# A cached-attention decode kernel: the last weight rows on eight DMA engines by the GpSimd queue, and values that trail keys by three groups

## The chip, the cores and the metric

One core of one Trainium2 chip runs the whole kernel. The metric is the device time of one execution in microseconds (us). The runs of the kernel before agree within 0.3%, so differences of a few tenths of a per cent need several rounds. The kernel before takes 195.49 us (median; 195.32 to 195.64).

Some words are used throughout. PE is the engine for matrix products (PEld in a profile is its loading of weights), DVE and ACT work on elements, GpSimd (POOL) is a fourth engine, and sync (SP) here only issues loads and stores. A *queue* is what an engine issues loads on (sync, activation, GpSimd). A *DMA engine* is one of the sixteen units that by the page move the bytes (in the kernel before a fetch puts one engine about 1.6 us behind).

## The reference, cut to what matters

```
B, D = 8, 448          # eight sequences, one token each
Hq, Hkv, Sk, Dh = 16, 8, 4096, 256
W = 1024               # the last 1024 cached positions count
q = x @ wq                                   # wq: 448 x 4096
p = softmax(q . k_cache[:, :, Sk-W:, :] * Dh**-0.5)
a = (p . v_cache[:, :, Sk-W:, :]) @ wo       # wo: 4096 x 448
b = gelu(layernorm(x) @ w1 + b1) @ w2 + b2   # w1: 448 x 1792
g = sigmoid((x * gate_w).sum(-1))
return g * a + (1 - g) * b
```

All is bf16. The keys and values that count are 2 x 33.5 MB, the weights some 10.6 MB; each byte is used once for eight tokens. So this is a kernel of loads.

## The kernel before

Keys and values are taken in 16 groups (u = 0 .. 15) of four heads; k15 stands for the keys of group 15, v13 for the values of group 13. A ring of nine 2 MB slots holds what is loaded; the sync queue fills the slots in the order of a plan, and a slot is filled again when its user is done.

```python
    RING = 9
    ...
    def kv_loader(src, u, parts):          # one 2 MB load, 128 partitions x 16 KB
        ...
                nc.sync.dma_start(t[:, i * n : (i + 1) * n], v[:, :, i * n : (i + 1) * n])
    ...
    # 448 rows = 3 x 128 + 64. The last 64 rows lie as half rows on all 128 partitions.
    wq_m = A_wq[0:DM, :].rearrange("(p r) n -> p (r n)", r=NR)
    wq_t = A_wq[DM:D, :].rearrange("r (h n) -> (r h) n", h=2)
    w1_m = B_w1[0:DM, :].rearrange("(p r) f -> p (r f)", r=NR)
    w1_t = B_w1[DM:D, :].rearrange("r (h n) -> (r h) n", h=2)
    ...
    add_kv("k", A_k_cache, 0, parts=2)
    add(("w1",), rows_loader([w1_m, w1_t]))
    add(("wq", 0), rows_loader([wq_m[:, 0 : 2 * HD]]))
    add(("wq", 1), rows_loader([wq_m[:, 2 * HD : 3 * HD], wq_t]))
    add(("w2",), rows_loader([w2_v]))
    for u in range(1, NQ - 1):
        add_kv("k", A_k_cache, u)
        if u < NQ - 2:
            add_kv("v", A_v_cache, u - 1)
    ...                                    # k15, v13, v14, v15, then wo in six pieces
```

In each group PE transposes the keys (`ktp`), ACT and DVE copy them out (`kt`), PE makes scores (`S_ps`), the softmax goes over DVE and ACT, PE multiplies the values (`PO`), and `finish` puts the result into `oT`. At the end `spread_rows` and `project` multiply by wo into `A_ps`:

```python
    spread_rows(0, HALF)
    values(u)              # u = 15
    finish(u)
    project(0)
    spread_rows(HALF, NHQ)
    for q in range(1, NHQ):
        project(q)
    ...                    # res = A_ps * g + mix, then the output
```

Of the kernel before, what the change touches and what calls it, by code (L numbers as in the profile page):

```python
# [11 lines left out]
BF16 = mybir.dt.bfloat16  # L12
# [5 lines left out]
def kernel(  # L18
# [15 lines left out]
    nc = tc.nc  # L34
# [14 lines left out]
    DM = NR * P  # L49
    DT = D - DM  # L50
    NF = F // P
    FH = F // 2
    HH = HD // 2
    QUAD = 4
    RQ = QUAD * rep
    NQ = NB * Hkv // QUAD
# [7 lines left out]
    NJ8 = HPQ * NJ  # L64
    WO_PARTS = [[(0, NJ8)]] * (NHQ - 1) + [[(0, 4), (4, 6), (6, 8)]]
    RING = 9
    BIG = 1e30
    qscale = float(Dh) ** -0.5

# [4 lines left out]
    consts = ctx.enter_context(tc.tile_pool(name="consts", bufs=1))  # L74
    ring = ctx.enter_context(tc.tile_pool(name="ring", bufs=RING))
    ktpool = ctx.enter_context(tc.tile_pool(name="ktpool", bufs=4))
    epool = ctx.enter_context(tc.tile_pool(name="epool", bufs=3))
    ps_s = ctx.enter_context(tc.tile_pool(name="ps_s", bufs=1, space=PSUM))
    ps_kt = ctx.enter_context(tc.tile_pool(name="ps_kt", bufs=3, space=PSUM))
    ps_sm = ctx.enter_context(tc.tile_pool(name="ps_sm", bufs=1, space=PSUM))  # L80
# [29 lines left out]

        return load

    def rows_loader(pieces):
        def load(t):
            o = 0
            for ap in pieces:
                n = 1
                for s in ap.shape[1:]:
                    n *= s
                dst = t[:, o : o + n]  # L120
                if len(ap.shape) == 3:
                    dst = dst.rearrange("p (a n) -> p a n", a=ap.shape[1])
                nc.sync.dma_start(dst, ap)
                o += n

        return load

# [7 lines left out]
        add((name, u), kv_loader(src, u, parts))  # L135

    wq_m = A_wq[0:DM, :].rearrange("(p r) n -> p (r n)", r=NR)
    wq_t = A_wq[DM:D, :].rearrange("r (h n) -> (r h) n", h=2)
    w1_m = B_w1[0:DM, :].rearrange("(p r) f -> p (r f)", r=NR)
    w1_t = B_w1[DM:D, :].rearrange("r (h n) -> (r h) n", h=2)  # L140
    w2_v = B_w2.rearrange("(p c) n -> p (c n)", c=NF)
    wo_v = A_wo.rearrange("(q p j) n -> p q (j n)", p=P, j=NJ8)

    add_kv("k", A_k_cache, 0, parts=2)
    add(("w1",), rows_loader([w1_m, w1_t]))
    add(("wq", 0), rows_loader([wq_m[:, 0 : 2 * HD]]))
    add(("wq", 1), rows_loader([wq_m[:, 2 * HD : 3 * HD], wq_t]))
    add(("w2",), rows_loader([w2_v]))
    for u in range(1, NQ - 1):
        add_kv("k", A_k_cache, u)  # L150
        if u < NQ - 2:
            add_kv("v", A_v_cache, u - 1)
    add_kv("k", A_k_cache, NQ - 1)
    for u in range(NQ - 3, NQ):
        add_kv("v", A_v_cache, u)
    for q in range(0, NHQ, 2):
        add(
# [11 lines left out]
        return slots[index[key]]  # L169

    x_sb = consts.tile([NB, D], BF16)
    pump()
    nc.scalar.dma_start(x_sb[:], xf)
    gw_b = consts.tile([NB, D], BF16)
# [5 lines left out]
    nc.scalar.dma_start(b2_r[:], B_b2.rearrange("(o d) -> o d", o=1))  # L180
    nc.scalar.dma_start(b1_sb[:], B_b1.rearrange("(p c) -> p c", c=NF))

    ident = consts.tile([P, P], BF16)
    make_identity(nc, ident[:])
    ones_f = consts.tile([P, P], F32)
    nc.gpsimd.memset(ones_f[:], 1.0)

# [2 lines left out]
    PO = ps_po.tile([P, Dh], F32)  # L190
    nc.vector.memset(PO[:], 0.0)

    NX = NR + 2
    DQ = D // QUAD

    def quads(ps):
# [2 lines left out]
            for i in range(QUAD)  # L199
        ]  # L200

    xz = consts.tile([NB, 2, P], BF16)
    yz = consts.tile([NB, 2, P], BF16)
    nc.vector.memset(xz[:], 0.0)
    nc.vector.memset(yz[:], 0.0)
    xT = consts.tile([P, NX, NB], BF16)
# [13 lines left out]
    def transposed(dst, src, srcz):  # L220
        tp = ps_misc.tile([P, NX, NB], BF16, tag="misc", name="tp")
        for r in range(NR):
            nc.tensor.transpose(tp[:, r, :], src[:, r:DM:NR], ident[:NB, :NB])
        for h in range(2):
            nc.tensor.transpose(tp[:, NR + h, :], srcz[:, h, :], ident[:NB, :NB])
        nc.vector.tensor_copy(dst[:], tp[:])

    for h in range(2):
        nc.vector.tensor_copy(xz[:, h, h::2], x_sb[:, DM:D])
    transposed(xT, x_sb, xz)  # L230
    nc.vector.reduce_sum(
        sel[:], ident[:].rearrange("p (a s) -> p s a", a=QUAD)[:, 0:RQ, :], axis=AXIS.X
# [19 lines left out]
    def norm_and_gate():  # L252
        stats = consts.tile([NB, nc.vector.BN_STATS_DIM], F32)
        nc.vector.bn_stats(stats[:], x_sb[:])
        mv = consts.tile([NB, nc.vector.BN_AGGR_DIM], F32)
        nc.vector.bn_aggr(mv[:], stats[:])
        eps_t = consts.tile([NB, 1], F32)
        nc.vector.memset(eps_t[:], 1e-5)
        rstd = consts.tile([NB, 1], F32)
        nc.scalar.activation(rstd[:], mv[:, 1:2], ACT.Sqrt, bias=eps_t[:], scale=1.0)  # L260
        nc.vector.reciprocal(rstd[:], rstd[:])
        y_sb = consts.tile([NB, D], BF16)
        nc.vector.tensor_scalar(
            y_sb[:],
            x_sb[:],
            scalar1=mv[:, 0:1],
            scalar2=rstd[:],
            op0=ALU.subtract,
            op1=ALU.mult,
        )  # L270
        for h in range(2):
            nc.vector.tensor_copy(yz[:, h, h::2], y_sb[:, DM:D])
        transposed(yT, y_sb, yz)
        prod = consts.tile([NB, D], F32)
        gl = consts.tile([NB, 1], F32)
        nc.vector.scalar_tensor_tensor(
            prod[:],
            in0=x_sb[:],
            scalar=1.0,
            in1=gw_b[:],  # L280
            op0=ALU.mult,
            op1=ALU.mult,
            accum_out=gl[:],
        )
        gth = consts.tile([NB, 1], F32)
        nc.scalar.activation(gth[:], gl[:], ACT.Tanh, scale=0.5)
        nc.vector.tensor_scalar(
            gg[:, 0:1], gth[:], 0.5, 0.5, op0=ALU.mult, op1=ALU.add
        )
        nc.vector.tensor_scalar(  # L290
            gg[:, 1:2], gth[:], -0.5, 0.5, op0=ALU.mult, op1=ALU.add
        )
        nc.vector.tensor_copy(
            spread[:, :, 0:NB],
            ident[0:NB, 0:NB]
            .rearrange("p (o b) -> p o b", o=1)
            .to_broadcast([NB, QUAD, NB]),
        )
        gp = ps_misc.tile([P, 2], F32, tag="misc", name="gp")
        nc.tensor.matmul(  # L300
            gp[:],
            lhsT=spread[:].rearrange("p i b -> p (i b)"),
            rhs=gg[:],
            start=True,
            stop=True,
        )
        nc.vector.tensor_copy(gg_s[:], gp[:])
# [24 lines left out]
    def query():  # L332
        qt = ps_misc.tile([P, Hq * NJ, NB], F32, tag="misc", name="qt")
        for r in range(NR + 1):
            w, o = slot("wq", r // 2), (r % 2) * HD
            for k in range(Hq * NJ):
                col = (k // NJ) * Dh + (k % NJ) * P
                half, c = divmod(col, HH) if r == NR else (0, col)
                nc.tensor.matmul(  # L339
                    qt[:, k, :],  # L340
                    lhsT=w[:, o + c : o + c + P],
                    rhs=xT[:, r + half, :],
                    start=(r == 0 and k == 0),
                    stop=(r == NR),
                    skip_group_check=True,
                )
        done(2)
        qv = qt[:].rearrange("p (g a i j) b -> p a j b g i", g=Hq // RQ, a=QUAD, i=rep)
        for a in range(QUAD):
            for j in range(NJ):  # L350
                nc.vector.tensor_scalar_mul(  # L351
                    qw[:, j, :, :, a, a * rep : (a + 1) * rep], qv[:, a, j], qscale
                )
# [39 lines left out]
    def bring(u):  # L393
        EB, selr = soft.pop(u)
        sm = ps_sm.tile([P, NCK + 1, RQ], F32, tag="sm", name="sm")
        nc.tensor.matmul(  # L396
            sm[:, 0:NCK, :], lhsT=perm[:], rhs=EB[:, :, 0:RQ], start=True, stop=True
        )
        nc.tensor.matmul(sm[:, NCK, :], lhsT=ones_f[:], rhs=selr[:], start=True, stop=True)  # L399
        ET = epool.tile([P, NCK, RQ], BF16, tag="ET", name="ET")  # L400
        nc.vector.tensor_copy(ET[:], sm[:, 0:NCK, :])  # L401
        rb = epool.tile([P, RQ], F32, tag="rb", name="rb")
        nc.vector.reciprocal(rb[:], sm[:, NCK, :])  # L403
        rsel = epool.tile([P, RQ], F32, tag="rsel", name="rsel")
        nc.vector.tensor_tensor(rsel[:], rb[:], sel[:], op=ALU.mult)
        soft[u] = (ET, rsel)

# [36 lines left out]
    def mlp_hidden():  # L444
        hT = ps_misc.tile([P, NF, NB], F32, tag="misc", name="hT")
        w = slot("w1")
        for r in range(NR):
            o = r * F
            for c in range(NF):
# [5 lines left out]
                    stop=False,  # L455
                    skip_group_check=True,
                )
        for h in range(2):
            for c in range(NF):
                nc.tensor.matmul(  # L460
                    hT[64 * h : 64 * h + 64, c, :],
                    lhsT=w[:, NR * F + c : NR * F + FH : NF],
                    rhs=yT[:, NR + h, :],
                    start=False,
                    stop=True,
                    skip_group_check=True,
                )
        done()
        z = consts.tile([P, NF, NB], F32)
        nc.vector.tensor_tensor(  # L470
# [45 lines left out]
    scores(0)  # L516
    top(0)
    mlp_out(hs)
    for u in range(1, NQ - 1):
        transpose_keys(u, steps(u - 1))  # L520
        if u < NQ - 2:
            values(u - 1)
        scores(u)
        top(u)
        if u < NQ - 2:
            finish(u - 1)
    u = NQ - 1
    transpose_keys(u, steps(u - 1))
    scores(u)
    top(u)  # L530
    values(u - 2)
    finish(u - 2)
    expo(u)
    turn(u)
    bring(u)
    values(u - 1)
    A_ps = ps_misc.tile([P, DQ], F32, tag="misc", name="A_ps")
# [34 lines left out]
    spread_rows(0, HALF)  # L572
    values(u)
    finish(u)
    project(0)
    spread_rows(HALF, NHQ)
    for q in range(1, NHQ):
        project(q)

    nc.vector.scalar_tensor_tensor(  # L580
# [40 lines left out]
```

## Time and profile before

| kernel before | |
|---|---|
| time | 195.49 us |
| bytes on the sync queue | 77.67 MB |
| share of the sixteen engines' span | 95.3% |
| PE busy, DVE busy | 76%, 58% |

The page of the profile (first the span, then the busy share of the DMA engines in 40 slices in tenths, then queues with packets, MB and share, then the chain of waits by engine):

```profile
span 193.7 us, 5200 instructions
...
DMA  5999999999999999999999999999999999999950
...
q1 hardware_dynamic: 6512, 77.67, 95.3%
q8 instruction: 18, 0.29, 0.6%
...
DMA 82%; PE 9%; ACT 3%; DVE 2%; issue 1%; SPq 1%; ACTq 0%
```

The reader is to see that the DMA engines are full from the second slice to the last but two. q8 is a queue of instruction fetches; it is small. The windows view (us of the window and its length, then the busy us of PE, PEld, DVE, ACT and POOL with the number of instructions, PE's clock, the DMA share and GB/s) says the same of mid-run, and shows the end:

```profile
80.00:120.00 40.00, 31.49 (x476) 22.44 (x475) 25.36 (x53) 19.78 (x24) 0.00 (x0) 1.00 1.01 426
...
180.00:186.00 6.00, 4.79 (x84) 3.40 (x76) 2.06 (x8) 0.00 (x0) 0.00 (x0) 0.50 0.95 382
186.00:194.00 8.00, 4.27 (x148) 3.94 (x148) 0.95 (x4) 0.00 (x0) 0.00 (x0) 0.50 0.17 59
```

The end in the timeline (start, us, engine, line, operation; in brackets what the engine had waited for):

```profile
183.30 0.23 DVE L440 CAST oT<-sm 128x16 bf16<-128x16 f32 x1 [0.94 <-PE sm L437]
...
187.11 0.92 PE L563 MATMUL A_ps<-slot,oP 128*8 128x112 bf16 x32
...
187.22 0.23 DVE L440 CAST oT<-sm 128x16 bf16<-128x16 f32 x1 [1.12 <-PE sm L437]
...
187.97 2.46 PE L563 MATMUL A_ps<-slot,oP 128*8 128x112 bf16 x96
...
190.48 0.33 DVE L580 SCALAR_TENSOR_TENSOR res<-A_ps,gg_s,mixb 128x112 bf16<-128x112 f32 x1 [1.92 <-PE A_ps L563]
```

The last group's result (`oT`) is ready at 187.2 + 0.2 us, and then PE runs the projection without a wait until 190.5.

One more reading is not a view of the page; it was worked out from the semaphore events in the packed trace. Each 2 MB load moves a semaphore by 16 steps as it lands, and the trace has the time of every step. The page counts sixteen engines, so one step is read here as one engine's landing (my reading; in e9 two loads split six and four ways took 6 and 4 steps). Then the sixteen steps of one load, sorted, say how far each engine is behind the first one. For 2 MB loads of the kernel before, us after the first step:

```
 at 19 us  0.00 0.06 0.07 0.07 0.10 0.13 0.19 0.22 0.38 0.41 0.45 0.49 0.62 0.64 0.93 1.91
 at 68 us  0.00 0.07 0.10 0.13 0.14 0.17 0.39 0.49 0.62 1.07 1.61 1.75 1.93 2.02 2.19 2.47
at 171 us  0.00 0.07 0.17 0.39 0.49 0.62 0.83 1.65 2.05 3.15 3.23 3.29 3.47 3.57 3.74 4.02
```

The engines start together and drift apart. From one line to the next several values have left the low group and come back about 1.6 us later. In the full list of loads, one such jump follows each packet of q8 (16,384 bytes, 1.08 us each) but the last, which came at 189.2 us. The steps don't tell which engine is which; that a value moved is read from what is missing in the next load's list. For the last but one piece of wo the first step is at 184.6 us and the last at 189.4, and the last step of all loads is at 190.0 us. PE waits for the *last* step: in e1 its last eight products waited for wo and started at 190.03 us, after a last step at 189.99; in the changed kernel at 191.49, after 191.44.

### The profile page before, as it was taken

The numbers are of one execution on the slowest core, as the hardware profiler recorded it, in microseconds if no ns is written. First come the engines' busy times: TensorE is split into PE (matmuls) and PEld (weight loads), VectorE is DVE, ScalarE is ACT, GpSimd is POOL, SyncE is SP. The second block draws the span as 40 slices with busy tenths as digits, with TensorE's granted clock in tenths as the row PEclk, the third lists the DMA queues.
The fourth block names the chain that finished last, engine by engine and source line by source line (L and its number), as shares of the span: only waits on it lengthen the run. The fifth ranks groups of instructions, "written<-read, shape, count | busy, mean of one in ns | idle before, by whom it ended". The sixth has DMA issues, their size and how long they took to land.

```text
span 193.7 us, 5200 instructions
## 1 busy us (share of the span) xinstructions
PE 148.1 (76%) x2334; PEld 110.3 (57%) x2334; DVE 112.9 (58%) x259; ACT 82.7 (43%) x101; POOL 0.8 (0%) x7
## 2 busy tenths in 40 slices
PE   1399967777778787878778787878868787984883
PEld 0399936555464646465637373737464646662672
DVE  7532344757475757584847575757565757786320
ACT  2352004536272728181808282828273636582000
POOL 1000000000000000000000000000000000000000
PEclk9998559999999999999999999999999999999555
DMA  5999999999999999999999999999999999999950
GB/s 203 397 437 415 430 431 428 426 426 416 420 423 430 426 426 423 430 430 423 425 423 423 430 423 416 428 430 420 426 426 430 420 433 420 423 433 404 414 217 10
DMA packets 6744, 78.02 MB, mean 403 GB/s; under 512 B 945, under 2 KB 1346, under 8 KB 1986
## 3 DMA queue, kind: packets, MB, share of 16 engines
q1 hardware_dynamic: 6512, 77.67, 95.3%
q8 instruction: 18, 0.29, 0.6%
q10 hardware_dynamic: 210, 0.02, 0.1%
q14 instruction: 4, 0.03, 0.0%
HBM read 77.68 MB, written 0.01 MB: 401 GB/s over the span
## 4 chain that ended last, share of the span: by engine, by line
DMA 82%; PE 9%; ACT 3%; DVE 2%; issue 1%; SPq 1%; ACTq 0%
DMA slot<-in_A_k_cache_dram 77%; DMA slot<-in_B_w_dram 5%; ACT kt L325 2%; PE S_ps L360 2%; PE ktp L322 2%; PE PO L420 2%; PE A_ps L563 2%; ACT E L380 1%; PE sm L437 1%; SPq L107 1%; DVE EB L388 1%; DVE nmx L372 1%; PE sm L399 0%; PE sm L396 0%; PE pp L547 0%
## 5 line engine op out<-in xcount | busy, mean ns | idle before, releaser
L325 ACT COPY kt<-ktp 128x1024 bf16<-128x1024 bf16 x64 | 63.2, 1017 | 82.2 <-PE ktp L322 82.2
L322 PE MATMUL ktp<-ident,slot 128*128 128x128 bf16 x1024 | 70.2, 224 | 22.1 <-ACT kt L325 11.4
L322 PEld LDWEIGHTS <-slot 128*128 128x128 bf16 x1024 | 63.7, 102 | 29.0 <-issue 15.7
L327 DVE COPY kt<-ktp 128x1024 bf16<-128x1024 bf16 x64 | 41.3, 685 | 15.8 <-PE ktp L322 15.6
L372 DVE TENSOR_REDUCE nmx<-S_ps 128x1 f32<-128x1024 f32 x16 | 19.6, 1225 | 22.3 <-PE S_ps L360 22.3
L360 PE MATMUL S_ps<-kt,qw 128*8 128x512 bf16 x256 | 32.3, 627 | 0.3 <-DVE qw L351 0.3
L388 DVE STREAM_TRANSPOSE EB<-E 128x1024 bf16<-128x1024 bf16 x16 | 19.9, 1245 | 6.7 <-ACT E L380 6.5
L420 PE MATMUL PO<-slot,ET 128*8 128x256 bf16 x512 | 18.5, 290 | 6.4 <-DVE ET L401 6.4
L380 ACT ACTIVATE E<-S_ps,nmx 128x1024 bf16<-128x1024 f32 x16 | 17.9, 1120 | 2.4 <-DVE nmx L373 2.4
L420 PEld LDWEIGHTS <-ET 128*8 128x8 bf16 x512 | 12.2, 90 | 10.5 <-DVE ET L401 8.7
L360 PEld LDWEIGHTS <-qw 128*8 128x8 bf16 x256 | 7.3, 95 | 12.0 <-issue 10.4
L401 DVE CAST ET<-sm 128x256 bf16<-128x256 f32 x16 | 6.7, 417 | 0.7 <-PE sm L399 0.7
L396 PE MATMUL sm<-EB,perm 128*128 128x256 bf16 x16 | 4.5, 280 | 1.6 <-DVE EB L388 1.6
L399 PE MATMUL sm<-selr,ones_f 128*128 128x8 f32 x32 | 5.5, 244 | 0.0
L440 DVE CAST oT<-sm 128x16 bf16<-128x16 f32 x16 | 3.5, 221 | 2.8 <-PE sm L437 2.8
L399 PEld LDWEIGHTS sm<-selr,ones_f 128*128 128x128 f32 x32 | 5.0, 196 | 0.1
L339 PE MATMUL qt<-xT,slot 128*128 128x8 bf16 x128 | 3.6, 168 | 0.4 <-DVE z L470 0.4
L339 PEld LDWEIGHTS <-slot 128*128 128x128 bf16 x128 | 3.6, 104 | 0.4 <-issue 0.3
L470 DVE TENSOR_TENSOR z<-hT,b_sb 128x112 f32<-128x112 f32 x1 | 0.3, 275 | 5.3 <-PE hT L460 5.3
L563 PE MATMUL A_ps<-slot,oP 128*8 128x112 bf16 x128 | 3.3, 294 | 0.0
L380 ACT ACTIVATION_READ_ACCUMULATOR E<-S_ps,nmx 128x1 f32 x16 | 3.2, 202 | 0.0
L403 DVE RECIPROCAL rb<-sm 128x8 f32<-128x8 f32 x16 | 3.2, 199 | 0.0
(122 smaller groups left out, 72.2 us busy)
## 6 DMA issues: line engine op xcount, KB each, us to landing
slot<-in_A_v_cache_dram SPq DMA_DIRECT2D x16, 2048.0 KB, 39.3
slot<-in_A_k_cache_dram SPq DMA_DIRECT2D x15, 2048.0 KB, 39.6
slot<-in_A_wo_dram SPq DMA_DIRECT2D x3, 896.0 KB, 32.0
slot<-in_A_k_cache_dram SPq DMA_DIRECT2D x2, 1024.0 KB, 7.2
slot<-in_A_wq_dram SPq DMA_DIRECT2D x1, 2048.0 KB
slot<-in_B_w_dram SPq DMA_DIRECT2D x1, 1568.0 KB
slot<-in_B_w_dram SPq DMA_DIRECT2D x1, 1344.0 KB, 10.1
slot<-in_A_wq_dram SPq DMA_DIRECT2D x1, 1024.0 KB
```

The lines of the kernel that those rows point to most:

```text
L322: nc.tensor.transpose(ktp[:, c, :], kn[:, o : o + P], ident[:])
L325: nc.scalar.copy(dst, ktp[:])
L327: nc.vector.tensor_copy(dst, ktp[:])
L339: nc.tensor.matmul(qt[:, k, :], lhsT=w[:, o + c : o + c + P], rhs=xT[:, r + half, :], start=(r == 0 and k == 0), stop=(r == NR), skip_grou ...
L360: nc.tensor.matmul(S_ps[32 * a : 32 * a + RQ, hf * CH * SK : (hf + 1) * CH * SK], lhsT=qw[:, j, b, half, a, :], rhs=KT[hf][:, j, :, a::QUA ...
L372: nc.vector.reduce_max(nmx[:], S_ps[:], axis=AXIS.X, negate=True)
L380: nc.scalar.activation(E[:], S_ps[:], ACT.Exp, bias=nmx[:], scale=1.0, accum_out=rowsum[:])
L388: nc.vector.transpose(EB[:].rearrange("p c r -> p (c r)"), E[:])
L399: nc.tensor.matmul(sm[:, NCK, :], lhsT=ones_f[:], rhs=selr[:], start=True, stop=True)
L401: nc.vector.tensor_copy(ET[:], sm[:, 0:NCK, :])
L420: nc.tensor.matmul(PO[32 * t : 32 * t + RQ, :], lhsT=ET[:, c, 0:RQ], rhs=vn[:, c * Dh : (c + 1) * Dh], start=(c < QUAD), stop=(c >= NCK - ...
L563: nc.tensor.matmul(dst, lhsT=oP[:, j, q, :], rhs=w[:, o + cols.start : o + cols.stop], start=(q == 0 and j == 0), stop=(q == NHQ - 1 and j ...
```

## The change

Intent: take the last 64 rows of wq and w1 from all sixteen engines and give them, as full rows, to eight engines, so that the engines end more evenly; and let the values trail the keys by three groups, so that the last group's softmax is done before its values and wo arrive.

```diff
+    LAG = 3
+    ER = P - DT                              # 64: rows on partitions 64 to 127
+    def step_over():                         # a tiny copy before each row load
+        ...
+        nc.gpsimd.dma_start(side[:, 2 * i : 2 * i + 2, 0:16], ...)
+
+    def ends(t, o, src):
+        n = src.shape[1]
+        for h in range(DT // 32):
+            rows = src[DM + 32 * h : DM + 32 * h + 32, :]
+            step_over()
+            nc.gpsimd.dma_start(
+                t[ER + 32 * h : ER + 32 * h + 32, o : o + n],
+                rows.rearrange("(j i) n -> i j n", i=NB),
+            )
 ...
-    add(("w1",), rows_loader([w1_m, w1_t]))
+    add(("w1",), rows_loader([w1_m], B_w1))
-    add(("wq", 1), rows_loader([wq_m[:, 2 * HD : 3 * HD], wq_t]))
+    add(("wq", 1), rows_loader([wq_m[:, 2 * HD : 3 * HD]], A_wq))
 ...
-    for u in range(1, NQ - 1):
+    for u in range(1, NQ):
         add_kv("k", A_k_cache, u)
-        if u < NQ - 2:
-            add_kv("v", A_v_cache, u - 1)
+        if u >= LAG:
+            add_kv("v", A_v_cache, u - LAG)
 ...
                 nc.tensor.matmul(
                     qt[:, k, :],
-                    lhsT=w[:, o + c : o + c + P],
-                    rhs=xT[:, r + half, :],
+                    lhsT=w[p0:P, c : c + P],  # p0 = 64 for the last rows
+                    rhs=xT[p0:P, r, :],
 ...
     finish(u)
-    project(0)
     spread_rows(HALF, NHQ)
-    for q in range(1, NHQ):
+    for q in range(NHQ):
         project(q)
```

Cut: the pools (`ET` and `rsel` get LAG + 1 buffers), the same order in the compute loop, and the layout of x to match the rows.

More of the change, by code (lines that the diff above doesn't have):

```diff
@@ L51 @@
     NF = F // P
-    FH = F // 2
-    HH = HD // 2
     QUAD = 4
@@ L76 @@
     ktpool = ctx.enter_context(tc.tile_pool(name="ktpool", bufs=4))
-    epool = ctx.enter_context(tc.tile_pool(name="epool", bufs=3))
+    epool = ctx.enter_context(tc.tile_pool(name="epool", bufs=2))
+    opool = ctx.enter_context(tc.tile_pool(name="opool", bufs=LAG + 1))
     ps_s = ctx.enter_context(tc.tile_pool(name="ps_s", bufs=1, space=PSUM))
@@ L111, in kv_loader, with rows_loader @@
         return load
-    def rows_loader(pieces):
+    side = consts.tile([NB, 8, 32], BF16)
+    turns = [0]
+    def step_over():
+        i = turns[0]
+        turns[0] += 1
+        nc.gpsimd.dma_start(
+            side[:, 2 * i : 2 * i + 2, 0:16],
+            xf[:, 0:32].rearrange("b (a n) -> b a n", a=2),
+        )
[4 more added lines that the diff above has]
+            step_over()
+            nc.gpsimd.dma_start(
+                t[ER + 32 * h : ER + 32 * h + 32, o : o + n],
+                rows.rearrange("(j i) n -> i j n", i=NB),
+            )
+    def rows_loader(pieces, tail=None):
         def load(t):
@@ L124, in load @@
                 o += n
+            if tail is not None:
+                ends(t, o, tail)
         return load
@@ L137 @@
     wq_m = A_wq[0:DM, :].rearrange("(p r) n -> p (r n)", r=NR)
-    wq_t = A_wq[DM:D, :].rearrange("r (h n) -> (r h) n", h=2)
     w1_m = B_w1[0:DM, :].rearrange("(p r) f -> p (r f)", r=NR)
-    w1_t = B_w1[DM:D, :].rearrange("r (h n) -> (r h) n", h=2)
     w2_v = B_w2.rearrange("(p c) n -> p (c n)", c=NF)
@@ L144 @@
     add_kv("k", A_k_cache, 0, parts=2)
-    add(("w1",), rows_loader([w1_m, w1_t]))
+    add(("w1",), rows_loader([w1_m], B_w1))
     add(("wq", 0), rows_loader([wq_m[:, 0 : 2 * HD]]))
-    add(("wq", 1), rows_loader([wq_m[:, 2 * HD : 3 * HD], wq_t]))
+    add(("wq", 1), rows_loader([wq_m[:, 2 * HD : 3 * HD]], A_wq))
     add(("w2",), rows_loader([w2_v]))
-    for u in range(1, NQ - 1):
+    for u in range(1, NQ):
         add_kv("k", A_k_cache, u)
-        if u < NQ - 2:
-            add_kv("v", A_v_cache, u - 1)
-    add_kv("k", A_k_cache, NQ - 1)
-    for u in range(NQ - 3, NQ):
+        if u >= LAG:
+            add_kv("v", A_v_cache, u - LAG)
+    for u in range(NQ - LAG, NQ):
         add_kv("v", A_v_cache, u)
@@ L171 @@
     x_sb = consts.tile([NB, D], BF16)
+    ident = consts.tile([P, P], BF16)
+    make_identity(nc, ident[:])
     pump()
@@ L181 @@
     nc.scalar.dma_start(b1_sb[:], B_b1.rearrange("(p c) -> p c", c=NF))
-    ident = consts.tile([P, P], BF16)
-    make_identity(nc, ident[:])
     ones_f = consts.tile([P, P], F32)
@@ L191 @@
     nc.vector.memset(PO[:], 0.0)
-    NX = NR + 2
+    NX = NR + 1
     DQ = D // QUAD
@@ L200, in quads @@
         ]
-    xz = consts.tile([NB, 2, P], BF16)
-    yz = consts.tile([NB, 2, P], BF16)
+    xz = consts.tile([NB, P], BF16)
+    yz = consts.tile([NB, P], BF16)
     nc.vector.memset(xz[:], 0.0)
@@ L223, in transposed, with ends_of @@
             nc.tensor.transpose(tp[:, r, :], src[:, r:DM:NR], ident[:NB, :NB])
-        for h in range(2):
-            nc.tensor.transpose(tp[:, NR + h, :], srcz[:, h, :], ident[:NB, :NB])
+        nc.tensor.transpose(tp[:, NR, :], srcz[:], ident[:NB, :NB])
         nc.vector.tensor_copy(dst[:], tp[:])
-    for h in range(2):
-        nc.vector.tensor_copy(xz[:, h, h::2], x_sb[:, DM:D])
+    def ends_of(dst, src):
+        nc.vector.tensor_copy(
+            dst[:, ER:P].rearrange("b (h i j) -> b h i j", h=DT // 32, i=NB),
+            src[:, DM:D].rearrange("b (h j i) -> b h i j", h=DT // 32, i=NB),
+        )
+    ends_of(xz, x_sb)
     transposed(xT, x_sb, xz)
@@ L270, in norm_and_gate @@
         )
-        for h in range(2):
-            nc.vector.tensor_copy(yz[:, h, h::2], y_sb[:, DM:D])
+        ends_of(yz, y_sb)
         transposed(yT, y_sb, yz)
@@ L335, in query @@
             w, o = slot("wq", r // 2), (r % 2) * HD
+            p0 = ER if r == NR else 0
             for k in range(Hq * NJ):
-                col = (k // NJ) * Dh + (k % NJ) * P
-                half, c = divmod(col, HH) if r == NR else (0, col)
+                c = o + (k // NJ) * Dh + (k % NJ) * P
                 nc.tensor.matmul(
                     qt[:, k, :],
-                    lhsT=w[:, o + c : o + c + P],
-                    rhs=xT[:, r + half, :],
+                    lhsT=w[p0:P, c : c + P],
+                    rhs=xT[p0:P, r, :],
                     start=(r == 0 and k == 0),
@@ L399, in bring @@
         nc.tensor.matmul(sm[:, NCK, :], lhsT=ones_f[:], rhs=selr[:], start=True, stop=True)
-        ET = epool.tile([P, NCK, RQ], BF16, tag="ET", name="ET")
+        ET = opool.tile([P, NCK, RQ], BF16, tag="ET", name="ET")
         nc.vector.tensor_copy(ET[:], sm[:, 0:NCK, :])
@@ L403, in bring @@
         nc.vector.reciprocal(rb[:], sm[:, NCK, :])
-        rsel = epool.tile([P, RQ], F32, tag="rsel", name="rsel")
+        rsel = opool.tile([P, RQ], F32, tag="rsel", name="rsel")
         nc.vector.tensor_tensor(rsel[:], rb[:], sel[:], op=ALU.mult)
@@ L457, in mlp_hidden @@
                 )
-        for h in range(2):
-            for c in range(NF):
-                nc.tensor.matmul(
-                    hT[64 * h : 64 * h + 64, c, :],
-                    lhsT=w[:, NR * F + c : NR * F + FH : NF],
-                    rhs=yT[:, NR + h, :],
-                    start=False,
-                    stop=True,
-                    skip_group_check=True,
-                )
+        for c in range(NF):
+            nc.tensor.matmul(
+                hT[:, c, :],
+                lhsT=w[ER:P, NR * F + c : NR * F + F : NF],
+                rhs=yT[ER:P, NR, :],
+                start=False,
+                stop=True,
+                skip_group_check=True,
+            )
         done()
@@ L518 @@
     mlp_out(hs)
-    for u in range(1, NQ - 1):
+    for u in range(1, NQ):
         transpose_keys(u, steps(u - 1))
-        if u < NQ - 2:
-            values(u - 1)
+        if u >= LAG:
+            values(u - LAG)
         scores(u)
         top(u)
-        if u < NQ - 2:
-            finish(u - 1)
+        if u >= LAG:
+            finish(u - LAG)
     u = NQ - 1
-    transpose_keys(u, steps(u - 1))
-    scores(u)
-    top(u)
+    expo(u)
+    turn(u)
     values(u - 2)
     finish(u - 2)
-    expo(u)
-    turn(u)
     bring(u)
```

## The prediction

"The upper eight" is the name for the eight engines to which the change gives the rows, "the lower eight" for the other eight. 1.9 us off every engine and 3.6 us on each loaded one, net +1.7, are from packet times of the trace before, and 195.49 less some 1.3 us of last lag (its 1.1 to 1.9) gives the 194.2.

> **What bounds the kernel now.** The sixteen DMA engines. The page gives the sync queue 77.67 MB and 95.3% of the engines' span; the windows view shows a DMA share of 0.99 to 1.03 from 10 to 180 us, PE about 80% busy; the chain of waits is 82% DMA. A 16,384-byte packet takes 0.614 us, 26.5 GB/s per engine.
>
> **The engines do not end together.** [...] From first to last step: 0.9 us for w1 (12 us), 2.5 us at 55 to 95 us, 4.0 us at 135 to 175 us, 4.9 us for a late wo piece (184.6 to 189.4). Seven engines stay within 0.8 us, eight end 3.2 to 4.9 us behind, one 2.1. The lags grow with the 16,384-byte packets of the instruction queue (18, 1.08 us each, one every 10 us); by the order in which they appear they visit eight engines in turn, about 1.6 us a visit. [...] The trace does not say which eight engines.
>
> **The end.** The last wo piece lands at 190.0 us; the 128 A_ps matmuls run without a gap from 187.1 to 190.45 us, because u=15's chain ends only at 187.2. DMA and compute end together; a gain needs both.
>
> **What the change does.**
> 1. The last 64 rows (229 + 524 KB, 47 KB per engine) leave the all-engine load: per engine 8 packets of 0.074 us and 8 of 0.160 us, 1.9 us less. They go as full rows to eight engines: 8 packets of 3,584 bytes (0.144 us) and 8 of 8,192 (0.308 us), 3.6 us, net +1.7. [...] If the fetch engines are the lower eight, their lags go from 3.2..4.9 to 1.3..3.0 us, the others from 0..0.8 to 1.7..2.6, the odd one to 3.8: the last lag falls by 1.1 to 1.9 us.
> 2. Values trail by three groups, so k15 lands one 2 MB load (4.9 us) earlier before the end, and u=15's chain (165.6 to 187.2 us) ends 3 to 4 us earlier. The first wo parts are projected before the last piece lands; about 0.4 us remains after it. Alone worth almost nothing; it lets item 1 show.
> 3. Fourteen fewer MLP matmuls: off the critical path, zero. Early k0 and w1 landings come up to 2 to 3 us later, and k1..k3 in a row make PE lag some 2 us a group; nine slots (44 us of loads) hide both.
>
> **Prediction.** 194.2 us (-0.7%), 8 in 10 between 193.1 and 195.7. Faster by over 2%: 0.03; within 2%: 0.94; slower by over 2%: 0.03. Perfect balance would gain only about 2.7 us (last lag 4.9 minus mean 2.1).
>
> **What would show it.** The spread of the late wo landings falls from 4.9 to 2.5 to 3.8 us, the last landing to about 188.5; u=15's chain ends near 183 to 184; A_ps matmuls wait for the last wo piece; the DMA share stays 1.0 in mid-run; 0.75 MB appear on a new queue.
>
> **What would make it wrong.** The fetch engines are the upper eight, or mixed: the spread grows to about 6.5 us and the time to about 197. [...] w1 comes late enough to empty the ring. A slot freed late in k1..k3 starves the DMA.

## The result, and the profile after

The changed kernel takes 197.08 us (196.94 to 197.20): ratio 1.0079, 95% interval 1.0064 to 1.0093, slower by 0.8%. All ratios here are the mean time of one kernel's runs over that of the kernel before in the same rounds, so not quite the ratio of the medians quoted.

The page after:

```profile
span 195.3 us, 5180 instructions
...
DMA  5999999999999999999999999999999999999830
...
q1 hardware_dynamic: 6224, 76.91, 93.3%
q0 software_dynamic: 384, 0.76, 1.0%
q8 instruction: 18, 0.29, 0.6%
...
DMA 86%; PE 8%; ACT 3%; issue 0%; SPq 0%; DVE 0%; ACTq 0%
```

The bytes are the same; 0.76 MB moved to a new queue, q0. The last slices fell from 9, 5 to 8, 3: engines go idle earlier at the end, yet the end is later. The windows view:

```profile
80.00:120.00 40.00, 32.39 (x496) 23.06 (x492) 25.90 (x53) 20.06 (x25) 0.00 (x0) 1.00 1.01 426
...
180.00:186.00 6.00, 4.11 (x100) 3.08 (x100) 1.42 (x5) 0.00 (x0) 0.00 (x0) 0.50 0.84 337
186.00:194.00 8.00, 3.35 (x107) 2.13 (x96) 0.33 (x1) 0.00 (x0) 0.00 (x0) 0.50 0.20 75
```

Mid-run is untouched (426 GB/s in both). From 180 to 186 us the DMA share fell from 0.95 to 0.84, and after 186 it rose: fewer engines work longer. The end in the timeline:

```profile
184.87 0.23 DVE L464 CAST oT<-sm 128x16 bf16<-128x16 f32 x1 [1.11 <-PE sm L461]
...
187.05 0.92 PE L583 MATMUL A_ps<-slot,oP 128*8 128x112 bf16 x32 [0.79 <-DMA slot<-in_A_wo_dram]
...
189.23 0.92 PE L583 MATMUL A_ps<-slot,oP 128*8 128x112 bf16 x32 [1.27 <-DMA slot<-in_A_wo_dram]
...
190.34 1.50 PE L583 MATMUL A_ps<-slot,oP 128*8 128x112 bf16 x32 [0.19 <-DMA slot<-in_A_wo_dram]
...
191.90 0.33 DVE L599 SCALAR_TENSOR_TENSOR res<-A_ps,gg_s,mixb 128x112 bf16<-128x112 f32 x1 [6.02 <-PE A_ps L583]
```

The last group's `oT` is now ready 2.3 us earlier, and PE waits for wo instead. But the last step of all loads came at 191.4 us instead of 190.0, and `res` started 1.42 us later. The steps of the changed kernel's loads show why (us after the first step):

```
 at 16 us  0.00 0.35 0.40 0.41 0.43 0.45 0.62 0.83 3.69 3.82 3.83 3.90 3.91 3.93 4.10 5.43
at 169 us  0.00 0.12 0.21 0.27 1.07 2.64 3.35 3.52 3.63 3.91 6.70 6.82 6.83 6.84 6.85 7.04
```

At 16 us, when the rows are in, there are two clean classes of eight, 3.6 us apart: the eight loaded engines are behind. By 169 us, six of the loaded ones have got another 3.1 to 3.4 us (6.70 to 7.04), two have not (3.63, 3.91); of the unloaded ones two have got about as much (3.35, 3.52). For the last but one piece of wo the spread is 8.3 us (182.6 to 190.9).

### The profile page after: what moved, and what is told of

It reads as the page before. It is cut to its first block, busy times and chain, and to the rows that moved or that the text cites. A ratio compares the mean times of both kernels' runs of the same rounds, so it can differ in the third digit from the quotient of the medians.

```text
span 195.3 us, 5180 instructions
## 1 busy us (share of the span) xinstructions
PE 148.5 (76%) x2318; PEld 110.5 (57%) x2318; DVE 112.2 (57%) x257; ACT 82.8 (42%) x101; POOL 5.4 (3%) x15
## 4 chain that ended last, share of the span: by engine, by line
DMA 86%; PE 8%; ACT 3%; issue 0%; SPq 0%; DVE 0%; ACTq 0%
DMA slot<-in_A_k_cache_dram 56%; DMA slot<-in_A_v_cache_dram 20%; DMA slot<-in_A_wo_dram 10%; PE ktp L346 5%; PE S_ps L384 2%; ACT kt L349 2%; ACT E L404 1%; PE PO L444 1%; PE sm L423 0%; PE A_ps L583 0%; DVE res L599 0%; PE sm L420 0%; SPq L145 0%; SPq L108 0%; ACTq L349 0%
## 5 line engine op out<-in xcount | busy, mean ns | idle before, releaser
L346 PE MATMUL ktp<-ident,slot 128*128 128x128 bf16 x1024 | 72.0, 227 | 21.2 <-ACT kt L349 10.6
L346 PEld LDWEIGHTS <-slot 128*128 128x128 bf16 x1024 | 66.0, 104 | 28.1 <-issue 15.7
L363 PE MATMUL qt<-xT,slot 128*128 128x8 bf16 (+1 forms) x128 | 3.8, 167 | 3.4 <-DMA slot<-in_A_wq_dram 3.4
L583 PE MATMUL A_ps<-slot,oP 128*8 128x112 bf16 x128 | 4.1, 291 | 2.5 <-DMA slot<-in_A_wo_dram 2.3
L363 PEld LDWEIGHTS <-slot 128*128 128x128 bf16 (+1 forms) x128 | 3.6, 104 | 3.6 <-DMA slot<-in_A_wq_dram 3.6
L583 PEld LDWEIGHTS <-oP 128*8 128x8 bf16 x128 | 2.9, 114 | 3.5 <-issue 3.5
L375 DVE TENSOR_SCALAR qw<-qt 128x32 bf16<-128x32 f32 x8 | 0.9, 180 | 5.2 <-PE qt L363 5.2
```

Of the source, the lines that this page charges most:

```text
L346: nc.tensor.transpose(ktp[:, c, :], kn[:, o : o + P], ident[:])
L363: nc.tensor.matmul(qt[:, k, :], lhsT=w[p0:P, c : c + P], rhs=xT[p0:P, r, :], start=(r == 0 and k == 0), stop=(r == NR), skip_group_check=True,
L583: nc.tensor.matmul(dst, lhsT=oP[:, j, q, :], rhs=w[:, o + cols.start : o + cols.stop], start=(q == 0 and j == 0), stop=(q == NHQ - 1 and j ...
```

## The experiments

Theory 1: sixteen engines must all end, the instruction fetches slow eight of them, and by the steps above six of these eight are among those that the change loads; the loss is imbalance. Rival 2: the later values cost the time (slots freed late, a longer end). Rival 3: the GpSimd queue itself costs time. Eleven kernels ran in five batches, each timed against the kernel before on the same chip, except the three probes, which got one look.

| run | what differs | time, us | ratio (95% interval) | last step of all loads, us |
|---|---|---|---|---|
| before | | 195.49 | | 190.0 |
| changed | | 197.08 | 1.0079 (1.0064, 1.0093) | 191.4 |
| e1 | later values only | 195.52 | 0.9995 (0.9983, 1.0007) | 190.0 |
| e2 | rows only | 197.20 | 1.0081 (1.0069, 1.0093) | 191.4 |
| e3 | no side copies | 196.85 | 1.0072 (1.0060, 1.0085) | 191.1 |
| e4 | side copies behind the rows | 198.96 | 1.0183 (1.0159, 1.0206) | 193.3 |
| e5 | as changed, rows by the sync queue | 198.86 | 1.0167 (1.0153, 1.0181) | 193.5 |
| e6 | as e5, rows on partitions 0 to 63 | 195.26 | 0.9995 (0.9982, 1.0009) | 189.7 |
| e10 | as e6, w1's rows only | 195.82 | 1.0012 (0.9999, 1.0026) | 189.7 |
| e11 | half the PE instructions (wrong result) | 193.29 | 0.9877 (0.9864, 0.9890) | 188.7 |

### e1 and e2: one half of the change at a time

e1 is the kernel before with LAG = 3, its pools and order, and the old row loads. e2 is the changed kernel with the old order and pools.

```diff
 # e1, against the kernel before            # e2, against the changed kernel
+        if u >= LAG:                       -        if u >= LAG:
+            add_kv("v", A_v_cache, u-LAG)  -            add_kv("v", A_v_cache, u-LAG)
 ...                                        ...
```

> Only the later values (LAG = 3, with its pools and the order at the end); the last rows stay on the sync queue as before. Theory 1 (the loss is the extra load on the wrong DMA engines): the last landing stays near 190 us as before, spread near 4.9 us, time 195.0 to 195.6 (ratio 0.997 to 1.000). Rival 2 (the later values cost the time, by slots freed late): about 197, ratio 1.007.

> Only the rows on eight engines of the GpSimd queue; values trail by one group as before. Theory 1: the last landing moves to about 191.4, spread about 8 us, time 197 or somewhat over it, because u=15's chain is late too (ratio 1.007 to 1.012). Rival 2: about 195.5, ratio 1.000.

e1 is the same as before, and e2 has the whole loss: rival 2 falls. e1's timeline shows why the later values bought nothing:

```profile
183.73 0.23 DVE L441 CAST oT<-sm 128x16 bf16<-128x16 f32 x1 [1.12 <-PE sm L438]
...
188.85 0.95 PE L561 MATMUL A_ps<-slot,oP 128*8 128x112 bf16 x24 [0.23 <-DMA slot<-in_A_wo_dram]
...
190.03 0.36 PE L561 MATMUL A_ps<-slot,oP 128*8 128x112 bf16 x8 [0.23 <-DMA slot<-in_A_wo_dram]
...
190.44 0.34 DVE L577 SCALAR_TENSOR_TENSOR res<-A_ps,gg_s,mixb 128x112 bf16<-128x112 f32 x1 [5.71 <-PE A_ps L561]
```

The last group is ready 3.5 us earlier than before (183.7 against 187.2), and all of that becomes waiting for wo: `res` starts at 190.44 instead of 190.48.

### e3 and e4: without the side copies, and with them behind the rows

```diff
 # e3: no side copies
-            step_over()
 # e4: the side copy behind each row load
-            step_over()
             nc.gpsimd.dma_start(t[ER + 32 * h : ...], ...)
+            step_over()
```

The rows stay on the GpSimd queue; e3 was meant to bring them to all engines alike, e4 to the other eight. That a side copy decides this was an assumption at this point.

> The changed kernel without the small side copies[...]. Theory 1: the two classes 3.6 us apart at the wq landing vanish, spread 4 to 5 us at the end, time 195.0 to 195.6 as with e1. Rival 3 (the GpSimd queue itself costs time, wherever its rows go): stays near 197.

> The side copies behind the row loads instead of before them[...]. If the instruction fetches visit exactly the eight engines that the change loads: spread under 4 us, time 193.5 to 194.3. If, as the landing lags of the changed kernel suggest (six of the eight loaded engines carry fetches, two or three of the eight others), they are mixed: two or three engines now end about 7 us late, the others less; time again about 197.

e3 was a miss for theory 1. The classes did vanish and the spread is 4.8 us as before, but the time stayed near the changed kernel's, as rival 3 said. e4 was worse than either guess. Another cost had to be there, and packet durations show it. Taking 26.6 GB/s as the undisturbed rate (16,384 bytes in 0.616 us), the packets that started between 4 and 30 us took longer than that by 0.36 us per engine before, 0.27 in the changed kernel, 1.78 in e3 and 3.86 in e4 (summed over packets above 1,500 bytes of the sync and GpSimd queues, divided by sixteen). Packets of 10,752 bytes had a mean of 0.405 us in the changed kernel, 0.529 in e3 and 0.552 in e4. So the changed kernel pays nothing of the kind; e3 and e4 do.

A new theory, at this point a guess that nothing had shown: it matters to which partitions an engine writes. The changed kernel, e3 and e4 all write the rows to partitions 64 to 127. If e3 and e4 do so with other engines than the changed kernel (0.27 us of stretch), the pairing of engines and partitions would be what costs 1.78 and 3.86 us.

### e5 and e6: the same eight-way split, two places in memory

Both use the sync queue, so that rival 3 can speak: no load goes by the GpSimd queue. Their edits leave the eight-way split alone, so I take both to load the same eight engines; the trace does not number them. In the two texts below, what stands about packets is what the pairing theory expects; if the place did not matter, e6 would come out as e5.

```diff
 # both
-            step_over()
-            nc.gpsimd.dma_start(
+            nc.sync.dma_start(
 # e6 alone
-    ER = P - DT                  # rows on partitions 64 to 127
+    ER = 0                       # rows on partitions 0 to 63
```

> The same row loads issued by the sync queue with an eight-way split [...], rows still on partitions 64 to 127. [...] packets of 10,752 bytes lengthen from 0.40 to about 0.55 us, time about 199 as e4. Rival (it is the GpSimd queue itself that stretched packets in e3 and e4): packets stay at 0.40 us, time 197 or less.

> As e5, but the rows on partitions 0 to 63. [...] no stretched packets (0.40 us), and the lower eight engines alone carry the rows; with two or three fetch engines among them the spread stays 7 to 8 us and the time 196.5 to 197.3. If the fetch engines all lie in the upper eight after all: spread about 3 us, time 193.5 to 194.5. [...]

The two differ in the partitions alone, and by 3.6 us. e5 has 3.95 us of stretch per engine, e6 0.18. In e5 it was the packets of 12,544 bytes that grew (0.645 us, against 0.472 in e6), not those of 10,752 as I had expected: by the sync queue the rows come later in the order. So the stretch is not the GpSimd queue's, and the pairing theory stands: the eight-way row loads of the sync queue write partitions 0 to 63 undisturbed (0.18 us) and 64 to 127 not (3.95 us); why, no trace here shows. If so, the changed kernel's rows, which stretch nothing on partitions 64 to 127 (0.27 us), are on other engines, as intended; the fetches below say the same. e4 is like e5 in stretch (3.86 and 3.95 us) and time (198.96 and 198.86 us), which speaks for the same eight in both. Rival 3 falls for the changed kernel too: its first engine ends only 0.24 us later by the GpSimd queue than that of e6 by the sync queue (first step of the last load at 183.17 and 182.93 us), and the two classes are 3.6 to 3.7 us apart in both.

e6 beats my number for it (196.5 to 197.3). Its steps at 176 us mirror the changed kernel's: 0.00 0.46, six from 3.14 to 3.48, and for the loaded ones 3.71 3.72 3.77 3.81 4.62 5.81 6.88 6.89. Now two loaded engines carry fetches and end 6.9 us behind, but the seventeenth fetch (183.5 us) falls on an unloaded one, where in the changed kernel it fell on a loaded one and made 7.0 into 8.3 us. That last step I had left out. The result is level with the kernel before, no more: the two loaded engines that carry fetches end last. Here two of the loaded engines carry fetches and six of the others, in the changed kernel six and two: so I take the loaded eight here to be the other eight, the lower ones.

### e7, e8 and e9: which engines carry the fetches

Probes, one look each: the kernel before with fewer ring slots and extra loads into a tile that nobody reads, split over a chosen number of engines, so that each group of engines is behind by a known amount. For e8 and e9 the amounts were an estimate from the 0.614 us of a 16,384-byte packet in the trace before: four engines get eight packets (4.9 us), two get four (2.5 us), the rest none. That takes the four to be among the six, which was an assumption; which engines they are by number was another.

```diff
 # e7: 7 slots; 2, 4, .. 14 rows of 32 KB from the activation queue
 # e8: 8 slots; 24 and 16 rows of 16 KB from the sync queue, "(i j) n -> i j n"
 # e9: as e8, the source interleaved
+    for k, p0 in ((6, 0), (4, 32)):
+        nc.sync.dma_start(
+            mark[p0 : p0 + 4 * k, :],
+            wide[p0 : p0 + 4 * k, :].rearrange("(j i) n -> i j n", i=k),
+        )
```

> A probe, not a version: the kernel before with seven ring slots and seven extra loads of 32 KB rows on 2, 4, .. 14 partitions from the activation queue, into a tile that nothing reads. [...] Tracking which step each fetch of the instruction queue delays tells which eight engines carry the fetches. [...] Time over 200 us, outputs correct.

> A second probe, since e7 starved the queues and lost its marks: the kernel before with eight ring slots and two extra loads of 16 KB rows on the sync queue, split six ways (partitions 0 to 23) and four ways (32 to 47), four rows an engine[...]. [...] The third and fourth fetch (near 35 and 47 us; those that in e6 delayed loaded engines) will then add 1.6 us to engines of one of these groups[...]. [...] Time about 198 us, outputs correct.

> The second probe mended: in e8 the source rows were contiguous in both dimensions and the loads split twelve and sixteen ways (its landings show it) [...]. With the source interleaved as in e6 they split six and four ways[...]. The third and fourth fetch then add 1.6 us to two engines[...]. Time about 199 us, outputs correct.

e7 failed: 221.3 us; the marks were no longer to be read in its steps, and the 32 KB packets took 3.5 us each where the rate of other packets would give 1.2. e8 failed too (203.2 us): its two loads, whose source was contiguous, took 12 and 16 semaphore steps instead of 6 and 4. e9 (198.5 us), with the source interleaved, took 6 and 4 steps. Just before the marks two engines were at 1.28 and 1.95 us; behind them they stood at 6.13 (4.85 more: the group of four, marked by 4.9 us) and 4.38 (2.43 more: the group of two, marked by 2.45). The one at 4.38 went on to 5.99 with the eleventh fetch, the second round's third; the third fetch is therefore on one of the two. The fourth raised an engine of the unmarked group, and in e6 it delayed one of the lower eight. The one in the first group rose by about 0.7 to 1.0 us after the 8 KB packets of another instruction queue, not with a fetch. So the group of four carries no fetch, one of the group of two does, and the other seven fall on unmarked engines. This is inferred from a single run; which engines they are is left open.

### e10: a smaller share for e6's eight

The e6 layout for w1's rows alone, wq's rows as before.

> Only w1's last rows on the lower eight engines (partitions 0 to 63, sync queue), wq's as in the kernel before, values trailing by three groups. Worked out from the lags: every engine is relieved of 0.6 us, the lower eight get 1.15 us; six fetch engines of the upper half end 0.6 us earlier, the two of the lower half 0.55 us later. Balance theory: last landing near 189.4 us, time 194.9 to 195.1 (ratio 0.997). If it is all noise: 195.5.

A miss. The last step of all loads did come earlier (189.7 us), but the time did not follow (ratio 1.0012, interval 0.9999 to 1.0026). In its profile `res` starts 0.35 us earlier than before, and the output lands 0.4 us later. The trace shows where the time went: the sync queue's two stores of the output (first before, then e10) took longer to issue.

```profile
190.84 0.71 SPq L590 DMA_DIRECT2D out_dram<-res  x2
...
190.49 1.07 SPq L598 DMA_DIRECT2D out_dram<-res  x2
```

The last packet of the second one then started at 192.36 us, 0.3 us after its fellows and just as an 8,192-byte packet of another instruction queue ended (191.91 to 192.36 us). Why the second store was issued late the trace does not say, nor whether the other four runs ended in the same way; so the earlier landing is in favour of the balance theory, and the time does not test it.

### e11: half the fetches

All runs so far move bytes about. This one leaves every load as in e1 and takes away PE instructions. It computes the wrong thing: two of eight transposes in a tile, repeated by the copies, and eight of 32 value products. (It is no valid version.)

```diff
-                    for c in range(NC):              # 8 transposes
+                    for c in range(2):               # 2, repeated by the copy
 ...
-        for c in range(NCK):                         # 32 value products
+        for c in [*range(QUAD), *range(NCK - QUAD, NCK)]:
```

> Wrong result on purpose: e1 (loads exactly as there, values trailing by three groups) with 2 instead of 8 transposes a tile, the copies repeating them, and 8 instead of 32 value matmuls a group: 2,203 PE instructions instead of 4,507, all bytes and loads the same. Fetch theory (each 16,384-byte packet of the instruction queue costs one of eight DMA engines about 1.6 us): about 9 packets instead of 18, each of the eight engines visited once before the last loads; spread of the late wo landings 2 to 2.5 us instead of 4.9, last landing near 187.5, time 193.0 to 193.6 (ratio 0.988). Rival (the lagging engines are slow for another reason, or by the amount of data): spread stays near 4.9 us and the time at 195.5, since the DMA ends last in e1 too.

The time came out as written: 193.29 us, ratio 0.9877. The page's queue lines and, first for e1 and then for e11, its PE lines:

```profile
q1 hardware_dynamic: 6512, 77.67, 95.8%
q8 instruction: 9, 0.15, 0.3%
...
PE 148.9 (77%) x2334; PEld 111.1 (57%) x2334; DVE 112.6 (58%) x259; ACT 82.9 (43%) x101; POOL 0.9 (0%) x7
...
PE 111.3 (58%) x1182; PEld 65.9 (34%) x1182; DVE 111.3 (58%) x259; ACT 82.8 (43%) x101; POOL 0.9 (0%) x7
```

Nine fetches instead of eighteen with the same 77.67 MB, and the spread of the last but one piece of wo is 2.1 us instead of 4.9. (The traces count 4,668 PE instructions in e1 and 2,364 in e11, not 4,507 and 2,203. In e1 some 255 of them lie between one fetch and the next in the mean, in e11 some 266: so I take q8 to be PE's queue.) The steps of the last piece of wo, us after the first step:

```
 e1, 185.13 us  0.00 0.12 0.33 0.44 0.45 0.47 0.75 1.98 3.11 3.16 3.35 3.39 3.56 3.59 3.96 4.86
e11, 185.28 us  0.00 0.04 0.09 0.21 0.43 0.51 0.87 1.56 1.62 1.72 1.73 1.73 1.77 1.84 2.08 3.42
```

The first engines end at the same time in both (185.1 and 185.3 us), so it is not that fewer PE instructions made the loads faster in general; only the late engines are less late. The last landing was expected near 187.5 us and came at 188.7. In this run the ninth fetch started at 186.6 us and made one engine late between the last two pieces; without it the last step would be 185.28 + 2.08, 187.4 us. It is also the slowest of the six runs (194.22 us; the others 193.03 to 193.47).

Its timeline still ends in waits for the DMA:

```profile
188.74 0.36 PE L568 MATMUL A_ps<-slot,oP 128*8 128x112 bf16 x8 [1.54 <-DMA slot<-in_A_wo_dram]
...
189.15 0.33 DVE L584 SCALAR_TENSOR_TENSOR res<-A_ps,gg_s,mixb 128x112 bf16<-128x112 f32 x1 [7.44 <-PE A_ps L568]
```

In both, `res` starts 0.45 us after the last step of all loads (190.44 after 189.99, 189.15 after 188.70): the end follows the last engine. So what makes engines lag is the instruction fetches, and a program with fewer PE instructions ends earlier although its PE was not the limit. In e1, with the same loads and PE waiting in the same place, the end was 2.2 us later by the medians (195.52 against 193.29).

No version that is right beat the kernel before.

## Why the prediction was wrong

**Bound by the sixteen engines, which do not end together: right.** e11 shows the cause of the drift by halving the fetches.

**The size of the extra load: right.** I had 3.6 us of rows per loaded engine; the classes are 3.6 us apart, and the row packets in the trace are 0.272 us for 7,168 bytes (two rows) and a mean of 0.318 us for 8,192. The relief of 1.9 us shows in the first step of the last piece of wo, 183.2 us instead of 185.2, and the net of +1.7 in the last step, which moved by 1.4 us.

**"If the fetch engines are the lower eight": this is the step that failed.** I read from the intent of the change that the upper engines must be the free ones. Nothing in the trace before said so, and I wrote that it does not. Six of the eight fetch engines are among the upper eight: six of the loaded engines end 6.7 to 7.0 us behind at 169 us, and with the seventeenth fetch one ends 8.3 us behind, where I had expected a spread of 2.5 to 3.8. The prediction's last paragraph had the other branch, "the spread grows to about 6.5 us and the time to about 197"; the time is right (197.08), the spread is 8.3 us, because I moved only the last engine by 1.7 us and forgot that the first one moves by 1.9 us the other way. I gave that branch too little weight: my range ended at 195.7.

**Later values: mechanism right, worth nothing as said.** The chain of u=15 ended at 185.1 us, not at 183 to 184; in the changed kernel PE waited 0.81 us for v15 itself, whose last step came at 181.36 us, 7.1 us after its first. In e1 the chain ended at 184.0. The prediction said that it "lets item 1 show"; there was nothing to show, and e1 and e2 price it at zero.

**k1 to k3 in a row: right.** The sync queue's waits for PE rose, and the ring hid them (SPq is the sync engine as it issues loads). Before:

```profile
SPq L107 <- PE ktp L322: 4.0, 10, 0.4
```

After:

```profile
SPq L108 <- PE ktp L346: 25.5, 12, 6.0
```

The columns are total us, times and longest. With these waits six times as long, mid-run bandwidth is 426 GB/s in both.

**Not foreseen:** that it matters to which partitions an eight-way load writes (3.95 us of stretch in e5, 0.18 in e6). The change itself avoids that trap (0.27 us); e3 and e4 fell in it (1.78 and 3.86), and e5 and e6 were built on it.

## What to carry to other kernels

In this kernel of loads the end was set by the slowest DMA engine (`res` started 0.45 us after the last step in e1 and in e11), so look at the sixteen semaphore steps of the last loads and not at the mean bandwidth; a DMA share of 1.0 in mid-run hid 4 us of drift. Before you shift bytes between engines, find out which are late: an intent in the code is not evidence. Loading the half with two fetch engines won nothing (e6), loading the half with six lost 0.8%. Fewer PE instructions made a kernel 1.2% faster whose PE is idle a quarter of the time: with nine fetches instead of eighteen the spread of the late loads fell from 4.9 to 2.1 us (e11). And when you do split a load unevenly, try it at two places in memory and look at the length of the packets beside it: here the place alone made 3.95 us of stretch or 0.18 (e5, e6).
